# A transformer block, forward and backward: turning two chunks' attention outputs by DMA, two stores moved to ScalarE, and a new order

## The chip, the cores and the metric

The kernel runs on one core of a Trainium2 chip. The metric is the device time of one execution in microseconds. Three runs of the kernel before took 556.07, 557.82 and 574.06 us (median 557.82).

A core has five engines with a program each: TensorE (PE in the profile; its weight loads are PEld), VectorE (DVE), ScalarE (ACT), GpSimd (POOL) and SyncE (SP). They wait for each other by semaphores. A DMA is issued by SP, ScalarE or GpSimd and then carried out by 16 DMA engines.

## The reference

One pre-layernorm transformer block with 2048 positions of width 512, and the gradients of its input and six weights for a given output gradient. Attention has 32 heads of 16 and looks back at 8 positions, two apart. All tensors are bf16.

```python
def _A_ref(x, wqkv, wo):                       # S=2048, D=512, H=32, Dh=16, W=8, dil=2
    q, k, v = qkv of (x @ wqkv), by head
    idx = pos[:, None] - off[None, :]          # off = arange(8) * 2; masked where idx < 0
    logits = einsum("bhsd,bhswd->bhsw", q, k[idx]) * Dh ** -0.5
    attn = softmax(logits)
    o = einsum("bhsw,bhswd->bhsd", attn, v[idx])
    return o @ wo
def _B_ref(x, w1, b1, w2, b2):                 # F=1792
    return gelu(x @ w1 + b1) @ w2 + b2
def f(x, ...):
    h = x + _A_ref(layernorm(x), wqkv, wo)
    return h + _B_ref(layernorm(h), w1, b1, w2, b2)
outputs: f, and vjp(f)(grad_out): the gradients of x, wqkv, wo, w1, b1, w2, b2
```

(The first lines of `_A_ref` are shortened to words.)

## The kernel before, in words

**Tiling.** The 2048 positions are four chunks of 512 (chunk 0 to 3). A chunk's tile has 128 partitions and four blocks of 512. Three parts follow each other and overlap. Part 1 is the attention forward by chunk (`p1_ln`, `p1_qkv`, `p1_attn`, `p1_o`, `p1_h`). Part 2 is the feed-forward, forward and backward (`p2_h`, `p2_out`, `p2_dg`, `p2_bwd`). Part 3 is the attention backward (`p3_go`, `p3_dots`, `p3_bands`, `p3_gl1`) and the weight gradients (`wg_ffn`), whose long accumulations fill TensorE between the others.

**The attention output.** For each chunk `p1_o` gathers shifted rows of v by DMA and multiplies them on VectorE by the attention weights, in four bands (product `prbo`, L518). TensorE sums each band (`bsum`, L527), ScalarE evicts the sum into the tile `ost` (L532). `ost` has positions on the partitions; the projection by `wo` (in `p1_h`) needs it turned, as `oT`. A chunk number c in the tuple `FMO` decides how:

```python
            if m % 2 and c not in FMO:
                turn(ost, oT, m // 2, "o")
        if c in FMO:
            turned(ost, oT, "o")
```

`turn` makes eight 128x128 transposes on TensorE (L543), half a tile, and one copy of 1024 columns on ScalarE (L297). `turned` issues one DMA transpose of the whole tile on SP (L291, `xload`). `FMO` is empty, so all four chunks are turned by TensorE. Other tiles are turned by DMA already: `ln1T`, `ln2T`, `goT`, `ghT` and some `gqkvT`. After `wo`, TensorE's result is added to x on VectorE (`h`, L747), normalised (`ln2`, ScalarE L381) and turned into `ln2T`, which the first feed-forward matmuls of that chunk read.

**Wide and narrow matmuls.** Some matmuls write 32 partitions each and come in fours, one for each quarter of the array: the band sums (`S` as weights, L487 and L527) and the projection to q and k (L626). All other long ones write 128. `mmul` can split such a wide one (L270) into four narrow ones (L268). `emit` decides it from the order alone:

```python
                if o.cls == 4:          # a step of wide matmuls that may be split
                    run.append(i)
                else:
                    if prev == 1 and o.cls == 1:     # narrow before the run and behind it
                        quad.update(run)
                    run, prev = [], o.cls
```

A transposing step is neither class (0), so a run beside one stays wide.

**What sets the order.** The functions do not issue instructions; they record steps (`op`) with what they read and write. Two tables at the end of the file then fix everything: `ORDER` lists the steps in the order of issue, from which each engine takes its own, and `HOMES` gives each buffer's place in SBUF or PSUM. Each engine runs its steps strictly in that order. DMA issues count as steps of the issuing engine, so a DMA that waits for its source holds up the issues behind it on SP. Issues also wait until one of eight completion semaphores, shared by SP and ScalarE, is free again.

**The end.** `p3_gl1` ends the layernorm backward of a chunk: VectorE writes `gx` (L570), and four DMAs of 128 KB store it (L287, tag `gxst`), all on SP. The last weight gradients (`wgsq`, of wqkv) are evicted by ScalarE (L297) and stored by DMAs that ScalarE issues.

Of the kernel before, what the change touches and what calls it, by code (L numbers as in the profile page):

```python
# [13 lines left out]
ACT = mybir.ActivationFunctionType  # L14
# [145 lines left out]
def kernel(  # L160
# [798 lines left out]
    def p3_gl1(c):  # L959
# [20 lines left out]
        for j, ap in enumerate(perm_rows(gxf[c * CH:(c + 1) * CH, :])):  # L980
            store(None, lambda ap=ap: ap, gx, lambda j=j: gx()[32 * j:32 * j + 32], 128, tag="gxst")
# [201 lines left out]
FMO = ()  # L1183
# [115 lines left out]
)  # L1299


# [28 lines left out]
```

## Time and profile before

| | |
|---|---|
| Three runs | 556.07, 557.82, 574.06 us |
| The profiled execution | 557.15 us; its span, from the first to the last instruction, 555.4 us |
| TensorE | 539.7 us busy (97%), 5568 matmuls |
| VectorE | 494.2 us (89%) |
| ScalarE | 324.2 us (58%) |
| GpSimd | 32.4 us (6%) |
| Granted TensorE clock | 0.999 |
| DMA | 126.40 MB, 228 GB/s on average |
| HBM | 55.74 MB read, 35.21 MB written |

Busy time is a share of the span. The profile models the ends of matmuls, so that a busy TensorE need not be at its peak pace. The profile's views used below are: the page's busy shares; the windows (busy time of each engine in a stretch of the span); the groups of instructions by line (count, total, mean, and the idle time before them with what ended it); the waits (who waited for whom); the timeline; the DMA issues with the time from issue to landing; and the chain of work that ended last.

### The profile page before, as it was taken

What the parts mean: (1) busy time and instruction counts of PE and PEld (TensorE: products, weight loads), DVE (VectorE), ACT (ScalarE), POOL (GpSimd) and SP (SyncE); (2) the same over time, 40 slices, a digit from 0 to 9 for tenths busy, and PEclk for the clock granted to TensorE, in tenths of its full rate; (3) what the DMA queues carried; (4) which work ended last, traced back from release to release, by engine and by line L of the source; (5) the groups of instructions that cost most, each with busy time, mean ns of one, the idle gap of its engine ahead of it and who ended that gap; (6) DMA issues with size and microseconds to landing.
All of it is one profiled execution on the core that took longest, in us unless ns stands there. A gap on an engine that the chain in (4) does not pass through costs nothing. (4 is left out here: it accounts for less than half of the span.)

```text
span 555.4 us, 13067 instructions
## 1 busy us (share of the span) xinstructions
PE 539.7 (97%) x5568; PEld 268.9 (48%) x5568; DVE 494.2 (89%) x648; ACT 324.2 (58%) x503; POOL 32.4 (6%) x38
## 2 busy tenths in 40 slices
PE   7999999999999999999999999999999998999995
PEld 4655554444444444444444444455455554555442
DVE  7999999999999999889885877789879998999992
ACT  4998699887999794996131324042324556633531
POOL 1610100021001000000000000000010001000000
PEclk9999999999999999999999999999999999999999
DMA  8898998975499617298999989999999999778237
GB/s 265 218 289 251 395 368 236 199 228 185 97 268 281 179 34 167 77 152 221 199 210 184 194 183 187 295 212 271 240 357 374 305 335 372 318 272 162 52 72 199
DMA packets 195306, 126.40 MB, mean 228 GB/s; under 512 B 149744, under 2 KB 190896, under 8 KB 193200
## 3 DMA queue, kind: packets, MB, share of 16 engines
q1 hardware_dynamic: 189760, 82.06, 64.5%
q0 software_dynamic: 3312, 41.42, 19.2%
q10 hardware_dynamic: 2176, 2.10, 1.2%
q8 instruction: 43, 0.70, 0.5%
q14 instruction: 15, 0.12, 0.1%
HBM read 55.74 MB, written 35.21 MB: 164 GB/s over the span
## 5 line engine op out<-in xcount | busy, mean ns | idle before, releaser
L270 PE MATMUL ps<-goT,w2T 128*128 128x512 bf16 x224 | 53.6, 379 | 0.8 <-DVE h2s L828 0.5
L270 PE MATMUL ps<-w1T,xb 128*128 128x512 bf16 x224 | 52.9, 379 | 0.0
L270 PE MATMUL ps<-w,gl 128*128 128x512 bf16 x216 | 50.5, 379 | 0.0
L297 ACT CAST wgs<-ps 128x512 bf16<-128x512 f32 (+1 forms) x30 | 16.2, 558 | 57.4 <-PE ps L268 35.7
L270 PE MATMUL ps<-ln2T,w 128*128 128x512 bf16 x188 | 44.2, 379 | 0.7 <-DVE xb L856 0.3
L774 ACT ACTIVATE xb<-ps,b1c 128x512 bf16<-128x512 f32 x56 | 35.7, 692 | 12.8 <-PE ps L270 12.5
L856 DVE SCALAR_TENSOR_TENSOR xb<-xb,ps 128x512 bf16<-128x512 bf16 x56 | 36.6, 685 | 6.2 <-PE ps L270 5.6
L518 DVE TENSOR_TENSOR prbq<-Rq,cfq 128x4096 bf16<-128x4096 bf16 x16 | 36.0, 2288 | 5.0 <-PE ps L487 1.7
L479 DVE TENSOR_TENSOR prb<-got,vw 128x4096 bf16<-128x4096 bf16 x16 | 36.3, 2282 | 2.7 <-PE ps L487 1.4
L518 DVE TENSOR_TENSOR prbv<-Rv,cfv 128x4096 bf16<-128x4096 bf16 x16 | 36.1, 2283 | 2.7 <-PE ps L268 1.8
L518 DVE TENSOR_TENSOR prbk<-Rk,cfk 128x4096 bf16<-128x4096 bf16 x16 | 36.1, 2283 | 0.7 <-PE ps L527 0.7
L518 DVE TENSOR_TENSOR prbo<-Ro,cfo 128x4096 bf16<-128x4096 bf16 x16 | 35.9, 2288 | 0.4 <-DMA k_d<-tmk 0.2
L479 DVE TENSOR_TENSOR prf<-qt,kt 128x4096 bf16<-128x4096 bf16 x16 | 35.5, 2275 | 0.0
L270 PEld LDWEIGHTS <-w2T 128*128 128x128 bf16 x224 | 21.8, 98 | 27.4 <-issue 2.0
L270 PEld LDWEIGHTS <-xb 128*128 128x128 bf16 x224 | 21.9, 98 | 26.4
L270 PEld LDWEIGHTS <-gl 128*128 128x128 bf16 x216 | 20.8, 98 | 25.6 <-issue 1.6
L796 ACT ACTIVATE xb<-xb 128x2048 bf16<-128x2048 bf16 (+1 forms) x16 | 26.8, 1690 | 7.8 <-DVE xb L795 7.7
L626 PE MATMUL ps<-ln1T,wqk 128*32 128x512 bf16 x512 | 30.2, 383 | 0.0
L270 PEld LDWEIGHTS <-w 128*128 128x128 bf16 x188 | 18.1, 97 | 23.0 <-issue 2.5
L268 PE MATMUL ps<-wqkvT,gqkvT 128*32 128x512 bf16 x448 | 27.4, 379 | 1.7 <-ACT gqkvT L297 1.6
L777 ACT ACTIVATE gl<-xb 128x2048 bf16<-128x2048 bf16 (+1 forms) x16 | 26.8, 1697 | 0.0
L792 ACT ACTIVATE x<-xb 128x2048 bf16<-128x2048 bf16 (+1 forms) x16 | 26.6, 1690 | 0.0
(198 smaller groups left out, 1054.0 us busy)
## 6 DMA issues: line engine op xcount, KB each, us to landing
Ro<-v_d POOLq DMA_DIRECT2D x4, 2304.0 KB, 11.2
Rq<-k_d POOLq DMA_DIRECT2D x4, 2304.0 KB, 11.6
Rv<-go_d POOLq DMA_DIRECT2D x4, 2304.0 KB, 14.2
Rk<-q_d POOLq DMA_DIRECT2D x4, 2304.0 KB, 13.4
g_d<-gl SPq DMA_DIRECT2D x9, 512.0 KB, 3.5
gh_d<-xb SPq DMA_DIRECT2D x9, 512.0 KB, 3.4
w<-in_B_w_dram SPq DMA_DIRECT2D x2, 1792.0 KB, 15.0
out_dram<-wgs SPq DMA_DIRECT2D x13, 256.0 KB, 7.1
```

The source lines that it names most:

```text
L268: T.matmul(out[32 * a:32 * a + 32, :], lhsT=l[:, 32 * a:32 * a + 32], rhs=r, start=start, stop=stop, skip_group_check=True)
L270: T.matmul(out, lhsT=l, rhs=r, start=start, stop=stop, skip_group_check=True)
L297: fn = lambda: A.copy(out=ap(), in_=pap())
L479: op("DVE", tt_us(4096), lambda g=g, pr=pr: V.tensor_tensor(out=pr(), in0=ql()[:, g, :].unsqueeze(1).to_broadcast([P, W, 512]), in1=_sub(k ...
L518: V.tensor_tensor(out=pr().rearrange("p a j (d h) -> p a j d h", h=H), in0=_sub(R()[:, o0, 0:1], [[st, 2], [512, 4], [32, DH], [1, H]]), i ...
L626: T.matmul(ps()[32 * a:32 * a + 32, gg * 512:(gg + 1) * 512], lhsT=_sub(wq_()[:, dc, 0:1], [[DH, H]], sel * D + 4 * g + a), rhs=rhs, start ...
L774: op("ACT", act_us(512, 1), lambda f=f, ps=ps, xb=xb, f0=f0: A.activation(out=xb()[:, f - f0, :], in_=ps(), func=ACT.Identity, bias=b1c[:, ...
L777: op("ACT", act_us(N), lambda xb=xb, gl=gl: A.activation(out=fl(gl), in_=fl(xb), func=ACT.Gelu_apprx_tanh), r=[xb], w=[gl], tag="gelu", mo ...
L792: op("ACT", act_us(N), lambda xb=xb, x2=x2: A.activation(out=fl(x2), in_=fl(xb), func=ACT.Square), r=[xb], w=[x2], tag="x2")
L796: op("ACT", act_us(N), lambda xb=xb: A.activation(out=fl(xb), in_=fl(xb), func=ACT.Tanh, scale=GC), w=[xb], tag="tanh", mode=6)
L856: op("DVE", 0.61, lambda f=f, ps=ps, z=z, f0=f0: V.scalar_tensor_tensor(out=z()[:, f - f0, :], in0=z()[:, f - f0, :], scalar=1.0, in1=ps() ...
```

## The change

Three edits. `FMO` names chunks 1 and 3, so that their `ost` is turned by one DMA transpose each. Of chunk 3's four `gx` stores the second and the fourth are issued by ScalarE. `ORDER` and `HOMES` are new throughout (in each of the two chunks one DMA takes the place of two turns and two copies, so the program has six steps fewer and the numbers in the table mean other steps).

```diff
         for j, ap in enumerate(perm_rows(gxf[c * CH:(c + 1) * CH, :])):
-            store(None, lambda ap=ap: ap, gx, lambda j=j: gx()[32 * j:32 * j + 32], 128, tag="gxst")
+            store(None, lambda ap=ap: ap, gx, lambda j=j: gx()[32 * j:32 * j + 32], 128, q="ACT" if c == NC - 1 and j % 2 else "SP", tag="gxst")
...
-FMO = ()
+FMO = (1, 3)
...
 ORDER = (
-    8, 22, 0, 11, 12, 23, 1, 7, 10, 6, 9, 48, 364, 27, 13, 49, 50, 26, 51, 44, 61, 28, 2, 62, 40, 25, 3, 45, 29, 41, 24, 46, 52, 42, 43, 53, 363, 15,
+    8, 22, 23, 10, 0, 1, 9, 21, 12, 14, 15, 7, 18, 6, 48, 27, 26, 11, 49, 50, 28, 51, 61, 25, 2, 62, 29, 3, 19, 4, 24, 5, 467, 139, 52, 44, 53, 40,
...
 HOMES = (
-    1210, 96, 3159, 673, 2261, 2549, 1153, 1025, 2485, 2261, 2117, 336, 160, 3031, 2775, 224, 3031, 2967, 1665, 3095, 377, 1537, 2839, 160, 2912, 0,
+    1637, 449, 64, 673, 2261, 2549, 1153, 288, 2485, 2261, 2117, 272, 1989, 1985, 3031, 224, 3095, 1729, 3031, 416, 192, 128, 417, 2837, 737, 7, 673,
...
```

What this does to the engines is seen in their rows, here at three places. A row has the line, the instruction, what it writes and reads, and the size; the numbers in names tell buffers apart.

TensorE behind the last band sum of chunk 3's attention output (`prbo` and `S`), where the feed-forward stretch begins. Before, `w` is the first feed-forward weight, `w2T` the turned second one:

```order
L527 LDWEIGHTS S
L527 MATMUL ps<-prbo_41_2197,S 32x512
L270 LDWEIGHTS w_226_24_984
L270 MATMUL ps<-ln2T_533_38_2030,w_226_24_984 128x512
L270 LDWEIGHTS w_226_24_984
```

And now, at the same place:

```order
L527 LDWEIGHTS S
L527 MATMUL ps<-prbo_40_2261,S 32x512
L268 LDWEIGHTS w2T_29_1652
L268 MATMUL ps<-goT_25_1513,w2T_29_1652 32x512
L268 LDWEIGHTS w2T_29_1652
```

The matmuls behind the band sum were wide (L270) and are now narrow (L268). It stays so through the rest of the feed-forward part, up to the first narrow sums of part 3, since no transposing step stands between any more. Over the whole program the narrow matmuls go from 3728 to 6736, the wide ones from 1374 to 622, and the 128x128 ones from 400 to 368; PE's matmuls go from 5568 to 7792. The changes from wide to narrow or back, counted in the order, go from 46 to 32.

SP's queue about chunk 2's and chunk 1's `ln2T` (`w2T` are the turned weights, `goT` the turned output gradient, `k_d`, `q_d`, `g_d` stores to scratch). Before:

```order
L291 DMA_TRANSPOSE w2T_30_1496<-in_B_w_dram 128x4x448
L287 DMA k_d<-tmk_29_866 128x2x512
L287 DMA g_d_73<-gl_31_1721 128x2x512
L282 DMA xp_386_32_1568<-in_A_x_dram 32x4x512
L291 DMA_TRANSPOSE ln2T_478_34_1913<-ln_2_465_34_1879 128x16x128
L287 DMA k_d<-tmk_23_538 128x2x512
L1114 DMA r_d<-rtr 16x32
L291 DMA_TRANSPOSE ln2T_533_38_2030<-ln_1_520_37_2003 128x16x128
```

And now:

```order
L291 DMA_TRANSPOSE w2T_29_1652<-in_B_w_dram 128x4x448 x3
L1074 DMA k_d<-zrow 16x512
L287 DMA k_d<-tmk_28_1462 128x2x512
L291 DMA_TRANSPOSE oT_442_30_1903<-ost_35_1809 128x16x128
L291 DMA_TRANSPOSE ln2T_471_32_1975<-ln_2_457_30_1939 128x16x128
L287 DMA q_d<-tmq_30_1901 128x2x512
L287 DMA q_d<-tmq_32_1067 128x2x512
L287 DMA out_dram<-h2s_30_1937 128x1x512
L291 DMA_TRANSPOSE ln2T_522_37_2083<-ln_1_509_36_2056 128x16x128
```

Chunk 1's `oT` now comes from a DMA that stands right before chunk 2's `ln2T` and behind three of `w2T`'s four transposes.

ScalarE's last steps (`wgsq` is evicted and stored, `gx` is chunk 3's). Before:

```order
L287 DMA out_dram<-wgsq_36_6655 128x2x512
L297 CAST wgsq_14_7445<-ps 128x512
L287 DMA out_dram<-wgsq_14_7445 128x2x512
L297 CAST wgsq_6_7471<-ps 128x512
L287 DMA out_dram<-wgsq_34_7265 128x2x512
L297 CAST wgsq_6_7471<-ps 128x512
L287 DMA out_dram<-wgsq_6_7471 128x2x512
```

And now:

```order
L297 CAST wgsq_11_9673<-ps 128x512
L287 DMA out_dram<-gx_20_9623 128x1x512 x2
L297 CAST wgsq_7_9692<-ps 128x512
L297 CAST wgsq_11_9673<-ps 128x512
L287 DMA out_dram<-wgsq_11_9673 128x2x512
L297 CAST wgsq_7_9692<-ps 128x512
L287 DMA out_dram<-wgsq_7_9692 128x2x512
```

Two `gx` stores now stand on ScalarE before its last three evictions; SP's list of `gx` stores has 14 entries instead of 16.

200 rows, old and new, of tables (HOMES, ORDER) are left out of this document.

## The prediction

> **What bounds the kernel now.** I read the busy shares of the page first, then the stretches of the span, then who waits for whom.
>
> ```profile
> PE 539.7 (97%) x5568; PEld 268.9 (48%) x5568; DVE 494.2 (89%) x648; ACT 324.2 (58%) x503; POOL 32.4 (6%) x38
> PEclk9999999999999999999999999999999999999999
> 0.00:60.00 60.00, 57.17 (x724) 33.44 (x724) 55.03 (x78) 47.09 (x64) 15.40 (x15) 1.00 0.89 266
> 60.00:125.00 65.00, 61.34 (x649) 31.33 (x648) 62.68 (x74) 56.51 (x67) 5.04 (x5) 1.00 0.92 277
> 125.00:320.00 195.00, 193.82 (x1120) 87.75 (x1122) 174.24 (x328) 130.88 (x187) 3.92 (x3) 1.00 0.78 175
> 320.00:440.00 120.00, 119.61 (x1571) 62.06 (x1567) 101.06 (x68) 39.22 (x78) 4.31 (x8) 1.00 1.04 266
> 440.00:549.10 109.10, 107.40 (x1520) 54.31 (x1509) 101.16 (x104) 49.95 (x109) 3.70 (x7) 1.00 0.75 232
> ```
>
> TensorE is busy 97% of the span at the full granted clock. The stretches (columns: PE, PEld, DVE, ACT, POOL, clock, DMA share, GB/s) say where the rest is lost: 6.5 us of the first 125 (2.83 + 3.66), then 1.2 us in 195, 0.4 us in 120, 1.7 us in 109. After 125 us nothing but TensorE's own work sets the pace. Before it TensorE and VectorE are both nearly full, so a wait there can have either cause.
>
> A busy TensorE may still be slower than its pace, so I take the pace from the timeline of PE (start, length, and the count of matmuls merged into the row; successive starts give the pace).
>
> ```profile
> 49.29 2.81 PE L626 MATMUL ps<-ln1T,wqk 128*32 128x512 bf16 x48
> 52.04 0.62 PE L543 MATMUL ps<-ident,ost 128*128 128x128 bf16 x8
> 52.59 0.61 PE L487 MATMUL ps<-prf,S 128*32 128x512 bf16 x8
> ...
> 115.47 0.61 PE L543 MATMUL ps<-ident,ost 128*128 128x128 bf16 x8
> 115.92 1.46 PE L270 MATMUL ps<-w,gl 128*128 128x512 bf16 x6
> ...
> 147.58 0.61 PE L527 MATMUL ps<-prbo,S 128*32 128x512 bf16 x8
> 148.13 1.04 PE L270 MATMUL ps<-ln2T,w 128*128 128x512 bf16 x4
> 149.00 1.03 PE L270 MATMUL ps<-goT,w2T 128*128 128x512 bf16 x4
> ...
> 380.50 1.03 PE L270 MATMUL ps<-gw1in,ln 128*128 128x512 bf16 x4
> 381.46 0.62 PE L527 MATMUL ps<-prbq,S 128*32 128x512 bf16 x8
> ...
> 383.63 1.90 PE L268 MATMUL ps<-gw1in,ln 128*32 128x512 bf16 x32
> 385.36 0.60 PE L527 MATMUL ps<-prbq,S 128*32 128x512 bf16 x8
> ```
>
> Four wide matmuls (128 columns) take 0.87 us from 148.13 to 149.00, so 0.216 us each. Thirty-two narrow ones (32 columns) take 1.73 us from 383.63 to 385.36: 0.054 us each, and four of them 0.216, the same as the wide one they stand for. A turn, eight 128x128 transposes, takes 0.45 us (115.47 to 115.92). Where the width changes something more is lost: four wide ones take 0.96 us before narrow ones (380.50 to 381.46), 0.10 too many, and eight narrow ones 0.55 us before wide ones (147.58 to 148.13), 0.12 too many. I take 0.11 us per change of width. The program has 3728 narrow, 1374 wide, 64 half-length and 400 transposing matmuls; at these paces (0.11 for a half-length one) that is 201 + 297 + 7 + 22 = 527 us of the 548 between the first matmul (1.2) and the last. The other 21 us are 46 changes of width (5.1), the cold start, and waits.
>
> **The change part by part.**
>
> *Turns that leave TensorE.* Four turns go (two in chunk 1, two in chunk 3): 4 x 0.45 = **1.8 us** off a saturated engine. Their four copies on ScalarE go too:
>
> ```profile
> L297 ACT COPY oT<-ps 128x1024 bf16<-128x1024 bf16 x8 | 8.1, 1011 | 0.8 <-PE ps L543 0.7
> ```
>
> That is 4.0 us of ScalarE, which idles 42% of the span; I count nothing for it.
>
> *Fewer changes of width.* A turn is wide, and a run of wide matmuls is split into narrow ones only if nothing else stands between two narrow neighbours. Without the turns the new order has 32 changes instead of 46: 14 x 0.11 = **1.5 us**. The price is that 752 wide matmuls become 3008 narrow ones, nearly all of them in the feed-forward stretch (about 125 to 320 us). I count the conversion at zero, from the paces above. A row of the same stage and operands, split already, has no waiting in it either:
>
> ```profile
> L268 PE MATMUL ps<-ln2T,w 128*32 128x512 bf16 x144 | 8.6, 379 | 0.0
> L270 PEld LDWEIGHTS <-w2T 128*128 128x128 bf16 x224 | 21.8, 98 | 27.4 <-issue 2.0
> L268 PEld LDWEIGHTS <-gqkvT 128*32 128x32 bf16 x448 | 12.2, 97 | 14.1 <-ACT gqkvT L297 2.1 <-DMA gqkvT<-gks 0.6
> ```
>
> Loading 32 columns takes 97 ns, as long as loading 128 (98 ns). If the four loads of a split matmul ran one after another, they would take 4 x 97 = 388 ns, more than its 216; but 448 of them together occupy 12.2 us, 27 ns each, since they overlap. The cost lies between 0 (the streamed columns are the same, which excludes a gain) and 172 ns a piece; I take 0, because the measured rows are split ones. The Trainium skill states a rule against this change, in "TensorEngine Tiling (Array Packing)", Restrictions and Gotchas: column tiling excludes the fast weight load. The equal 97 and 98 ns agree with it. By that rule alone, with loads in series, the sum would become 683 us; by the trace's pace it is unchanged.
>
> *Two DMA transposes that come in.* Chunk 1's and chunk 3's tile is now turned on SP's queue, and the `wo` matmuls wait for the landing. The changed order puts 30 wide equivalents (6.5 us) between chunk 1's last band sum and `wo`, and 36 (7.8 us) for chunk 3. ScalarE's eviction of that sum comes first:
>
> ```profile
> L532 ACT ACTIVATE ost<-ps 128x512 bf16<-128x512 f32 x16 | 9.3, 599 | 1.4 <-PE ps L527 1.4
> ln2T<-ln SPq DMA_TRANSPOSE x3, 4.3
> ghT<-ghr SPq DMA_TRANSPOSE x4, 9.0
> gqkvT<-gqs SPq DMA_TRANSPOSE x1, 11.9
> 352.97 13.57 DMA ghT<-ghr
> ```
>
> The same shape lands 4.3 us after issue for ln2T, which is turned in this very stretch, and 13.57 us after it in the worst case of the trace (the chain, at 353 us, with the DMA engines full). With 0.6 for the eviction, 4.9 us fits under 6.5 and 7.8: no wait. With 13.57 the waits are 7.7 and 6.4 us. I take zero, since ln2T is nearest in place; both ends are kept. A gain below zero is excluded, as these matmuls stood behind the turns before. Behind the new issue on SP stands chunk 2's ln2T, whose source, the normalised rows, comes later on ScalarE than the turned tile's last eviction; so the queue does not hold it up; behind chunk 3's stand w1T's, first needed well after that `wo`. The two transposes move 1 MB more, at a DMA share of 0.78 to 0.92 there.
>
> *The last stores.*
>
> ```profile
> 545.86 5.67 SPq L287 DMA_DIRECT2D out_dram<-gx  x6
> ...
> 549.50 0.58 ACT L297 CAST wgsq<-ps 128x512 bf16<-128x512 f32 x1 [1.14 <-PE ps L270]
> 550.12 0.38 ACTq L287 DMA_DIRECT2D out_dram<-wgsq  x1
> DMA to landing us min/median/max: 2.4/2.5/3.7
> ```
>
> SP issues its last gx store by 551.53, ScalarE its last wgsq store at 550.12, and stores land 2.4 to 3.7 us after issue. So both end between 552.5 and 554. Taking two of 16 issues from SP frees some 1.2 us there (0.6 each), but the wgsq store, which follows the last matmul, ends as late: I count 0, between -0.5 and +1. On ScalarE the two issues (0.38 each) stand before three evictions; the last one had waited 1.14 us for TensorE and so covers 0.76, if gx is ready. The Trainium skill's "DMA: Bandwidth & Descriptors", Issuing engines are not separate DMA queues, says a second issuing engine saves only the issuing time; with these rows that saving is hidden too, so rule and rows both give 0.
>
> *The new order elsewhere.* Its gain or loss is what becomes of TensorE's waits. Those that the view of waits lists on PE add up to about 8 us: these are the largest but for the start.
>
> ```profile
> PE ps L268 <- ACT gqkvT L297: 1.6, 1, 1.6
> PE ps L416 <- DVE ln L385: 1.5, 1, 1.5
> PE ps L270 <- DVE h2s L828: 1.4, 2, 0.9
> PE ps L416 <- ACT kt L297: 1.0, 1, 1.0
> ```
>
> They can go (-8) or double (+8). I take 0.
>
> **Sum.** The profiled execution took 557.15 us, 1.75 beyond its span of 555.4 and 0.7 below the median shown (557.82). 557.15 - 1.8 - 1.5 = **553.9 us**.
>
> **The rivals.**
>
> *VectorE paces the first stage (555.8).* Up to 145 us it lacks little:
>
> ```profile
> DVE st L360 <- DMA xt<-in_A_x_dram: 1.7, 1, 1.7
> DVE nm L376 <- POOL rstd L373: 1.6, 3, 0.9
> ```
>
> If TensorE's savings there only make it wait for VectorE's products, 9 of the 14 changes of width (1.0 us) and chunk 1's turns (0.9) are given back: 553.9 + 1.9. For it: VectorE's work is the same as before. Against it: the loss of 6.5 us there has other causes as well.
>
> *The turned tiles land late, and the kernel is slower (558.8 to 568).* It decides from a landing of 5.9 us for chunk 1 and 7.2 for chunk 3; from 8.2 us for both the two waits eat the gain of 3.3. With ghT's median of 9.0 they are 3.1 and 1.8: 553.9 + 4.9 = 558.8; with 13.57 they are 14.1: 568. For it: the DMA share of 0.92, and w2T's transposes queued just ahead on SP. Against it: ln2T's 4.3.
>
> *The split matmuls do not keep pace (683).* 752 x 0.172 = 129 us more. Only the single load time speaks for it.
>
> *The early waits shrink as well.* Half of the 8 us gone gives 549.9, all of it 545.9.
>
> **How the numbers follow.** Forecast 0.60 (own range 551.5 to 556), VectorE 0.15, late tiles 0.12, shrinking waits 0.10, split matmuls 0.03. Two per cent, about what a measurement of this kernel can tell from no change, is 546.0 and 568.3 around 557.15. Below lies only the far end of the shrinking waits, with 0.05 for what the new order may do unseen; above lie the split matmuls and the worst landings, 0.05. The range from 548 to 562 leaves out the tails of both, under 2 in 10.
>
> **What would show it.** Right: PE's transposing rows of ost fall from 64 to 32; the narrow pace in 125 to 320 us stays at 0.054 us with no idle time; PE's `wo` rows wait for no oT transpose; the last matmul starts some 3 us earlier; what follows it stays near 6 us. Wrong: a PE wait on oT of over 2 us, a pace of 0.058 or more in the feed-forward stretch (0.004 x 4 x 900 matmuls is 14 us, the 2% alone), or waits in the first 145 us that differ by more than 3 us from 6.5. What I cannot read from the profile is how a wholly new order meets the DMA queue early on: that would make the prediction wrong first.

## The result, and the profile after

The changed kernel took 562.42 us (median of 20 runs, 558.06 to 569.32), the kernel before 556.91 in the same comparison (20 runs, 553.87 to 574.06): a ratio of **1.0059**, 95% interval 1.0035 to 1.0084. A second comparison gave 565.71 against 556.00, 1.0118 (1.0064 to 1.0172). So the change costs 0.6 to 1.2%, where 0.6% less was forecast. The changed kernel's own times stand in two groups, 558 to 564 and 566 to 569 us, and the profile below is of an execution of 567.36 us. The ratios and intervals, here and below, leave out runs more than 1.5% above the fastest of their kernel (of the changed kernel the whole upper group); the medians count all.

The page of the changed kernel (busy shares, granted clock, instruction queue), then its stretches in the columns of before (length, PE, PEld, DVE, ACT, POOL, clock, DMA share, GB/s):

```profile
PE 541.3 (96%) x7792; PEld 286.5 (51%) x7792; DVE 496.4 (88%) x648; ACT 321.8 (57%) x499; POOL 25.2 (4%) x38
PEclk9999999999999999999999999999899999999999
q8 instruction: 61, 1.00, 0.8%
```

```profile
0.00:60.00 60.00, 55.88 (x709) 35.45 (x710) 55.57 (x76) 45.77 (x63) 8.54 (x15) 1.00 0.88 267
60.00:125.00 65.00, 63.14 (x736) 32.66 (x734) 62.46 (x74) 55.52 (x66) 4.67 (x5) 1.00 0.98 268
125.00:320.00 195.00, 188.45 (x3247) 98.98 (x3249) 171.28 (x329) 131.17 (x190) 3.94 (x3) 0.99 0.84 177
320.00:440.00 120.00, 113.35 (x1437) 58.54 (x1433) 91.00 (x61) 31.43 (x58) 3.78 (x7) 0.99 1.04 252
```

The first 125 us lost 6.5 us of TensorE before and lose 5.98 now. The loss is new, and later: 6.55 us in 125 to 320 us (1.2 before) and 6.65 in 320 to 440 (0.4 before). A shorter execution (561.01 us, gx_all_SP below) still loses 6.97 and 4.02 there. The view of waits on PE names what ended them (total, times, longest), and the timeline shows the two longest (idle time before a row, and its releaser, in brackets):

```profile
PE ps L487 <- ACT wgs L297: 4.2, 1, 4.2
PE ps L268 <- DVE xb L856: 3.7, 2, 3.3
PE ps L487 <- DVE prb L479: 1.8, 2, 1.0
```

```profile
266.13 1.90 PE L268 MATMUL ps<-w1T,xb 128*32 128x512 bf16 x16 [3.33 <-DVE xb L856]
...
386.30 0.54 POOL L471 DMA_DIRECT2D Rv<-go_d  x1 [38.66 <-ACT got L297]
386.44 1.60 SPq L287 DMA_DIRECT2D out_dram<-wgs  x3
...
398.54 0.58 ACT L297 CAST wgs<-ps 128x512 bf16<-128x512 f32 x1 [8.79 <-DMA out_dram<-wgs]
399.17 0.62 PE L487 MATMUL ps<-prb,S 128*32 128x512 bf16 x4 [4.16 <-ACT wgs L297]
```

Each of the two costs more than its length. Right behind it the granted clock is about half (third column from the right), though the page's row of tenths hardly shows it:

```profile
266.20:269.60 3.40, 3.40 (x36) 1.43 (x39) 3.30 (x6) 3.13 (x3) 0.00 (x0) 0.53 0.76 259
399.20:402.60 3.40, 3.40 (x36) 1.46 (x39) 2.29 (x1) 0.62 (x2) 0.00 (x0) 0.51 0.77 205
```

TensorE is busy for all of the 3.40 us, and by the clock 1.6 us of them are lost each time, on top of waits of 3.33 and 4.16. The Trainium skill's "TensorE: Matmul & The Clock Gate", Part 1: The HAM clock gate, says that the array falls to half its clock after an idle window of about 3.4 us and gets it back after as long a busy one. The 3.4 us agree; but the window need not be idle here, as the last section shows from all profiles.

### The profile page after: what moved, and what is told of

It is laid out like the page before. It is cut to its first block, busy times and chain, and to the rows that moved or that the text cites. A ratio compares the mean times of both kernels' runs of the same rounds, so it can differ in the third digit from the quotient of the medians.

```text
span 565.6 us, 17518 instructions
## 1 busy us (share of the span) xinstructions
PE 541.3 (96%) x7792; PEld 286.5 (51%) x7792; DVE 496.4 (88%) x648; ACT 321.8 (57%) x499; POOL 25.2 (4%) x38
## 4 chain that ended last, share of the span: by engine, by line
PE 41%; DMA 5%; DVE 4%; SPq 2%; ACT 1%; issue 0%; DVEq 0%; ACTq 0%
PE ps L268 22%; PE ps L270 14%; PE ps L527 3%; DMA out_dram<-wgs 2%; DMA ln1b<-ln_d 2%; DVE prbv L518 2%; SPq L291 1%; DVE prb L479 1%; PE ps L543 1%; DMA tmgod<-got 1%; DVE prbk L518 1%; PE ps L487 1%; ACT got L297 0%; PE ps L919 0%; DVE h L755 0%
## 5 line engine op out<-in xcount | busy, mean ns | idle before, releaser
L268 PE MATMUL ps<-w1T,xb 128*32 128x512 bf16 x896 | 53.0, 383 | 3.5 <-DVE xb L856 3.3
L268 PE MATMUL ps<-goT,w2T 128*32 128x512 bf16 x832 | 52.0, 379 | 1.1 <-DVE xb L856 0.4
L268 PE MATMUL ps<-w,gl 128*32 128x512 bf16 x776 | 46.2, 384 | 0.0
L268 PEld LDWEIGHTS <-xb 128*32 128x32 bf16 x896 | 26.2, 98 | 26.5 <-issue 4.6
L268 PEld LDWEIGHTS <-w2T 128*32 128x32 bf16 x832 | 24.4, 97 | 22.6 <-issue 2.2
L561 ACT ACTIVATE gyr<-ps,rstd 128x512 bf16<-128x512 f32 x16 | 10.9, 680 | 39.4 <-PE ps L268 39.4
L268 PEld LDWEIGHTS <-gl 128*32 128x32 bf16 x776 | 23.0, 98 | 20.2 <-issue 1.4
L268 PE MATMUL ps<-ln2T,w 128*32 128x512 bf16 x512 | 31.1, 379 | 0.6 <-DMA w<-in_B_w_dram 0.3
L268 PE MATMUL ps<-gor,gw2in 128*32 128x512 bf16 x416 | 24.8, 379 | 0.7 <-DMA gw2in<-g_d 0.7
```

The source lines that it names most:

```text
L268: T.matmul(out[32 * a:32 * a + 32, :], lhsT=l[:, 32 * a:32 * a + 32], rhs=r, start=start, stop=stop, skip_group_check=True)
```

## The experiments

All were timed beside the kernel before; medians in us, and the ratio to before with its 95% interval:

| kernel | median | before | ratio |
|---|---|---|---|
| again (the changed kernel) | 565.71 | 556.00 | 1.0118 (1.0064–1.0172) |
| gx_all_SP | 566.36 | 556.00 | 1.0147 (1.0104–1.0190) |
| woT_copy_later | 569.30 | 556.00 | 1.0229 (1.0179–1.0279) |
| wgs_home | 571.80 | 556.00 | 1.0274 (1.0241–1.0306) |
| store_before_gather | 563.48 | 555.72 | 1.0115 (1.0088–1.0142) |
| store_and_woT | 564.95 | 555.72 | 1.0150 (1.0093–1.0208) |
| change_in_old_order | 573.53 | 555.72 | 1.0270 (1.0211–1.0329) |
| long_run_wide | 556.95 | 555.72 | 1.0009 (0.9981–1.0038) |
| split_in_old_kernel | 558.62 | 556.00 | 1.0043 (1.0023–1.0062) |
| split_first_part | 557.23 | 556.00 | 1.0034 (1.0010–1.0059) |
| split_last_part | 560.41 | 556.00 | 1.0093 (1.0062–1.0124) |
| cut_by_columns | 562.39 | 556.68 | 1.0102 (1.0066–1.0138) |
| wide_store_copy | 556.47 | 556.00 | 1.0007 (0.9979–1.0034) |
| wide_store_copy_junk | 554.87 | 556.68 | 0.9985 (0.9953–1.0017) |
| old_order_wide | 568.69 | 556.68 | 1.0199 (1.0167–1.0230) |
| four_waits_wide | 554.31 | 555.87 | 0.9970 (0.9954–0.9986) |
| four_waits_split | 563.71 | 555.87 | 1.0102 (1.0065–1.0140) |

**First theory: the waits of the new order.** Nothing edited, and the stores on ScalarE undone:

> The changed kernel once more, nothing altered; its times so far lie between 558 and 569 us, and the profile that we have is of an execution of 567.4. Theory A (waits of the new order): TensorE waits 3.66 us at 262 us for VectorE's xb products and 4.48 us at 395 us behind an eviction that waits for a weight gradient store, and runs at half rate for about 2.5 us after each; an execution of about 559 us should show the same two waits, and be shorter because one or both stay below the length from which the half rate follows, or because the clock granted elsewhere is higher. Theory B (the parts of the change themselves): a shorter execution shows neither wait, and is still 2 us or more above the kernel before; then the loss is spread over the narrow matmuls or the tail.

```diff
-... q="ACT" if c == NC - 1 and j % 2 else "SP", tag="gxst")
+... tag="gxst")
```

> The changed kernel with all four of the last chunk's input gradient stores issued by SyncE again; order and homes as in the changed kernel. Theory A: the stores on ScalarE are worth nothing, so the time stays within 1 us of the changed kernel. Theory B: the two stores on ScalarE cost (or gain) 2 us or more, and the time moves by that.

The second profile of the changed kernel (568.94 us) has the waits at 262 and 395 us again, 3.3 and 5.1 us. With all stores on SyncE the profiled execution took 561.01 us; it has the first wait, but not the second. There the store was issued ahead of the gather:

```profile
384.06 1.64 SPq L287 DMA_DIRECT2D out_dram<-wgs  x3
384.64 0.54 POOL L471 DMA_DIRECT2D Rv<-go_d  x1 [38.66 <-ACT got L297]
392.32 0.58 ACT L297 CAST wgs<-ps 128x512 bf16<-128x512 f32 x1 [4.24 <-PE ps L268]
```

It landed at 388.63, 4.6 us after issue; in the changed kernel it was issued 0.14 us behind the gather and landed with it, 12.0 us later (398.46 and 398.11). The time of the kernel can't be told from the changed one's (566.36 and 565.71 in one comparison).

**Two of the waits taken apart.** ScalarE's copy moved back, and another place for one staging buffer:

```diff
 ScalarE: sums of goT, tanh, tanh
-COPY woT<-woR          (ahead of them)
+COPY woT<-woR          (behind the last tanh)
 SyncE:   ... gh_d<-xb, gh_d<-xb
+DMA_TRANSPOSE xw2in<-gl (was ahead of these two)
```

> The changed kernel with ScalarE's 4.04 us copy of woT, which starts at 257.06 us between the small steps that VectorE waits for, moved behind the third tanh step that follows it, into ScalarE's idle stretch of 7.69 us (269.3 to 277.0); one transposing load of gl that takes over its source's place moves with it. Theory A: VectorE no longer sits 2.73 us at 263.3 behind ScalarE, TensorE's wait of 3.66 us at 262 us shrinks below 1 us and the half rate after it goes, so the kernel gains 3 to 6 us on the changed one (553 to 556 us). Rival: VectorE was late by its own load, the wait stays at 2.5 us or more, and the time stays within 1.5 us of the changed kernel.

```diff
 HOMES, entry of one wgs buffer
-2085
+0
```

> The changed kernel with one staging buffer of the weight gradients (the one that ScalarE fills at 398.5 us) in another place of SBUF, so that it no longer waits for the store of the buffer that lay there (issued at 386.4, landed at 398.5 us). Theory A: ScalarE's 8.8 us wait and TensorE's 4.48 us behind it go, with the half rate after it: a gain of 4 to 7 us (552 to 555 us). Rival: the gather issued at 386.3 us, which lands at 398.1, is what really holds that stretch: TensorE then waits for VectorE's products or ScalarE's taps at the same place, and less than 1.5 us is gained.

Both kernels became slower, as neither theory had it. The waits aimed at went, and what stood behind them was worse. In the first, VectorE now waited for the transfer that had moved along, whose source its next junk output overwrites; in the second it waited for the same late store, whose place it now shared (views of waits on VectorE, one row of each kernel):

```profile
DVE jk L564 <- DMA xw2in<-gl: 6.4, 1, 6.4
```

```profile
DVE cfv L497 <- DMA out_dram<-wgs: 12.8, 1, 12.8
```

TensorE waited 6.4 us at 269 us and 8.2 us at 418 us instead. In both it was then VectorE that waited for a transfer. So the store was moved on its queue:

```diff
 SyncE
+out_dram<-wgs
 DMA_TRANSPOSE gw1in<-gh_d   (2.41 us)
-out_dram<-wgs
```

> The changed kernel with one weight gradient store (the 256 KB one that lands last at 398.5 us in the profile after) moved one place ahead on SyncE's queue, before the transposing load that holds that queue for 2.41 us, so that it is always issued ahead of the 2304 KB gather that GpSimd issues at 386.3 us. Theory A: whether this store is issued just before or just after the gather makes the two groups of the changed kernel's times: 384.06 before 384.64, landed after 4.6 us, in an execution of 561.0 (the kernel with all stores on SyncE); 386.44 after 386.30, landed after 12.0 us, in one of 567.4. Then all times here lie at 558 to 561 us and TensorE waits less than 1 us at 394 to 400 us. Rival: the two groups come from the clock; then times of 565 and more stay as frequent as they are in the changed kernel (about half).

> The kernel with the store ahead of the gather, and ScalarE's 4.04 us copy of woT in its idle stretch as in woT_copy_later, but with the transposing load that takes its source's place put behind the small loads of r_d on SyncE's queue, so that nothing which VectorE needs stands behind it (there VectorE sat 6.4 us for them). Theory A: TensorE's wait of 3.65 us at 262 us goes together with the half rate after it (1.5 to 2.6 us): 552 to 556 us, 3 to 6 below store_before_gather. Rival: VectorE is late by its own work there and at least 2 us of the wait stay: within 2 us of store_before_gather.

In store_before_gather TensorE no longer waits at 394 us, but the times still reach from 558 to 575 us: the rival's side, as far as the times go. Its profile (563.68 us) has a wait of 3.3 us at 418 us, for the next pair of that kind: a store of go_d, issued 0.39 us ahead of the next gather, landed 11.8 us later. (The row there names a store of wgs; in wide_store_copy_junk, where the same eviction waits, it names that of go_d.) store_and_woT missed likewise: VectorE waited 7.5 us for xw2in<-gl once more. Over all profiles the first pair is consistent: in each of the nine in which the store of wgs was issued first, TensorE did not wait for that eviction; in each of the five in which the gather was (the changed kernel twice, and later woT_copy_later, long_run_wide and split_first_part), it waited 3.5 to 5.1 us. In long_run_wide the way is longer: behind the gather the issue of a transposing load took 8.80 us, and the store stood behind it on SyncE's queue. (wgs_home, where that eviction no longer waits for the store, is left out.)

**The change without its order, and without its split.**

```diff
-FMO = ()
+FMO = (1, 3)
+... q="ACT" if c == NC - 1 and j % 2 else "SP", tag="gxst")   (order of before, 20 steps of chunk 1 moved back)
```

> The kernel before with the change's two named parts alone: the attention outputs of chunks 1 and 3 turned by a DMA transpose in place of TensorE, two of the last four input gradient stores issued by ScalarE. Order and places are those of before, but for 20 steps of chunk 1 that follow its turned tile (its DMA, the four output projections, the additions and layer norm behind them), which stand some 20 to 40 places later, so that the 4 to 7 us of the DMA have cover. Theory A: the parts are worth what the prediction said, the order is what lost it: 551.5 to 554.5 us where before has 556. Rival: the parts themselves cost: 556 us or more.

```diff
-                    if prev == 1 and o.cls == 1:
+                    if prev == 1 and o.cls == 1 and len(run) < 100:
```

> The changed kernel, in which the one long run of 188 matmul steps (125 to 320 us) that was split into narrow matmuls is left wide: 752 matmuls of 128 columns in place of 3008 of 32. Theory A: the split costs nothing, and the time stays within 1.5 us of the changed kernel (two more changes of width, 0.2 us). Rival: 3008 small matmuls hold TensorE up (their instructions, their weight loads): the time falls by 3 us or more.

In both the rival held. The parts, in the old order and with the 20 steps moved, cost 2.7%. And leaving one run wide, which I had counted at nothing twice, brought the changed kernel back to the kernel before: 1.0009. The split became the main suspect, and came next: in the kernel before, in each part of the run, and cut in another direction.

```diff
 split_in_old_kernel (in before)
-                    if prev == 1 and o.cls == 1:
+                    if (prev == 1 or at[i] == 1190) and o.cls == 1:
 split_first_part, split_last_part (in after)
-                        quad.update(run)
+                        quad.update(x for x in run if len(run) < 100 or at[x] < 1030)     (last: >= 1030)
```

> The kernel before, order and places untouched; only its long run of 163 wide matmul steps (652 matmuls, behind the last turn of chunk 3's outputs up to the first part 3 sums, some 165 to 330 us) is split into 2608 narrow ones, as the changed kernel's long run is. Theory C (the split costs, not by TensorE's own pace but by DMA: in the changed kernel the transposing loads at 264 to 336 us land after a median of 5.6 to 6.0 us, in the same kernel with the run left wide after 4.7 to 4.9, and the queue that brings instructions moves 61 packets in place of 42): 2 to 5 us slower than before, with later transposing loads in that stretch. Rival, my prediction's step: the pace of four narrow matmuls is that of one wide, so within 1 us of before.

> The changed kernel in which the long run of 188 steps is narrow in its first 120 steps (125 to about 260 us) and wide in the last 68. Theory C: SyncE's queue is not the limit there (its transfers have gaps), so the time is that of the kernel with the run left wide, 556 to 558 us. Rival D: every narrow matmul costs the same somewhere on TensorE or its weight loads, so 120 of 188 steps cost 64% of what the split costs (2.4 of 558.8 against 556.9 in the shorter runs, 5 to 6 by the medians): 558 to 561 us.

> The same the other way round: the first 120 steps wide, the last 68 (about 260 to 320 us, where SyncE issues transposing loads one behind the other) narrow. Theory C: nearly the whole cost of the split, 559 to 563 us. Rival D: 36% of it, 557.5 to 559 us.

The split costs 0.43% in the kernel before, whose order and places are untouched. In the changed kernel its first 120 steps cost nothing that can be told (557.23 against 556.95 with the run wide; 1.0034 and 1.0009) and its last 68 cost 3.5 us (560.41). A price per matmul would have put 64% on the first part, so that rival is out; the cost sits where SyncE issues transposing loads back to back. There the loads land later (issues of 264 to 336 us in the wide kernel, the changed kernel, and split_last_part; count, median us to landing; ahead of them the queues' packets, MB, and share of 16 engines):

```profile
q1 hardware_dynamic: 52051, 14.41, 102.5%
q8 instruction: 3, 0.05, 0.3%
xw1in<-xb SPq DMA_TRANSPOSE x4, 4.8
ghT<-ghr SPq DMA_TRANSPOSE x3, 4.7
vw<-v_d SPq DMA_TRANSPOSE x2, 4.7
```

```profile
q1 hardware_dynamic: 48353, 13.47, 113.2%
q8 instruction: 10, 0.16, 1.0%
xw1in<-xb SPq DMA_TRANSPOSE x4, 5.3
ghT<-ghr SPq DMA_TRANSPOSE x3, 5.6
vw<-v_d SPq DMA_TRANSPOSE x2, 5.6
```

```profile
q8 instruction: 9, 0.15, 0.9%
xw1in<-xb SPq DMA_TRANSPOSE x4, 6.3
ghT<-ghr SPq DMA_TRANSPOSE x3, 6.4
vw<-v_d SPq DMA_TRANSPOSE x2, 5.0
```

The split kernels move less in more time, and their instruction queue brings 9 or 10 packets there in place of 3. Groups of three or four scatter (the kernel before has 5.4 for its xw1in), but the mean of all transposing loads issued in this stretch, 16 to 18 in each kernel, sorts all nineteen profiles: 4.6 to 4.9 us in the seven in which the stretch is wide, 5.0 to 5.7 in the twelve in which it is split.

Who pays for it can be read too (waits on VectorE, the changed kernel, then the wide one, whose list has no `tmgod`):

```profile
DVE prb L479 <- DMA xw1in<-xb: 3.0, 1, 3.0
DVE u L566 <- DMA tmgod<-got: 2.4, 1, 2.4
```

```profile
DVE prb L479 <- DMA xw1in<-xb: 0.3, 1, 0.3
```

SyncE issues the first of these `tmgod` at 329.73 us in place of 325.01. In the nine profiles of the new order with the last part narrow, VectorE waits 2.1 to 3.4 us for `tmgod`, and TensorE 0.7 to 2.8 for VectorE's `prb` in the same stretch; of the five with it wide four have at most 0.5 and none, one (four_waits_wide, below) 1.8 and 1.1. split_in_old_kernel has later loads (5.05 us in the mean, before 4.80) but no such wait: where its 2.4 us go is not shown, and its profile is of a run of 556.58 us, below its median.

Is it the number of instructions, or the narrow tile?

```diff
 cut_by_columns: the last 68 steps, four matmuls each
-T.matmul(out[32 * a:32 * a + 32, :], lhsT=l[:, 32 * a:32 * a + 32], rhs=r, ...)
+T.matmul(out[:, 128 * a:128 * a + 128], lhsT=l, rhs=r[:, 128 * a:128 * a + 128], ...)
```

> The kernel split_last_part with another cut: the last 68 steps of the long run (260 to 320 us) are again four matmuls each in place of one, but cut along the 512 moving columns (four times 128 x 128 weights on 128 columns), so that the array stays full width; the first 120 steps are wide. As many more instructions as in split_last_part. Theory C1 (the number of instructions that TensorE must be brought delays the transposing loads): the loads land after 5 to 6.4 us as there, and the time is 559 to 563 us, of which 1.6 us are the slower pace itself (4 x 0.0555 us against 0.2158, 272 times). Theory C2 (narrow tiles themselves): loads at 4.4 to 5.0 us as in the kernel left wide, 557 to 559 us.

In this kernel some partial sums of those steps are not kept; number and size of the instructions are as described. Its time, 562.39 us less 1.6 for the pace (an estimate, from 0.0555 us a piece against a quarter of 0.2158), is near that of split_last_part (560.41), and its loads land as late (means 5.2 and 5.2 us):

```profile
q8 instruction: 9, 0.15, 0.9%
xw1in<-xb SPq DMA_TRANSPOSE x4, 5.3
ghT<-ghr SPq DMA_TRANSPOSE x3, 6.1
vw<-v_d SPq DMA_TRANSPOSE x2, 5.4
```

So the number of instructions delays the loads, not the narrow tile (C1). That it costs the whole time is likely from the times but not shown by this trace: its profile, of 560.09 us, has no wait of VectorE for `tmgod` and 1.4 us for xw1in. By which path the instructions delay the loads is not shown either: that their packets stand in the loads' way on the DMA engines fits the rows, but was not tried by itself. The Trainium skill's "DMA: Bandwidth & Descriptors", Queues, rings and completion order, says that an engine takes turns between queues a whole packet at a time; a packet of instructions here holds 16 KB (1.00 MB in 61). No run here isolates that.

**The old order again, with the run wide.** The edit is that of long_run_wide in change_in_old_order.

> The kernel change_in_old_order (the change's two parts in the order of before, 573.5 us) with its long run left wide. The split was worth 2.4 us in the kernel before. Theory: 569 to 572 us, and the waits for the turned tiles (5.0 and 4.6 us and the half rate after them) remain, so it is they, not the split, that make that kernel slow. Rival: the split is the main cost there too: 560 us or less.

568.69 us, as expected: the split is the smaller part there. TensorE waits for the turned tile of chunk 3 and for chunk 1's layer norm, which my edit had delayed along with its turned tile:

```profile
PE ps L270 <- DMA ln2T<-ln: 6.1, 2, 5.9
PE ps L270 <- DMA oT<-ost: 5.7, 2, 4.2
```

So the new order does buy something: cover for chunk 3's turn at least; the wait for the layer norm comes at least in part from my own edit.

**The waits taken away together.** With the run wide:

```diff
 ScalarE
-COPY woT<-woR
 c x4, sums of goT x2, tanh
+COPY woT<-woR
```

> The changed kernel with three edits: the long run left wide; the weight gradient store ahead of the transposing load on SyncE's queue (as in store_before_gather); and ScalarE's 4.04 us copy of woT put between two small groups of its steps so that VectorE's next inputs (five 0.2 us steps, two sums, one 1.9 us tanh) come ahead of it, with no transfer moved past another that VectorE needs. If the three waits named so far are what the change lost: the wait of 3.4 us at 261 us shrinks below 1.5 us and the one at 390 us goes, 551 to 555 us, below both kernels. Rival: what is next late (VectorE's own load of 88%) takes the place of the wait, 556 to 558 us.

```diff
 HOMES, two jk buffers
-1409, 1825
+1841, 416
```

> The kernel wide_store_copy (556.5 us), in which VectorE sat 2.2 us at 267 us until a transposing load had read a tile whose place its next junk output takes; the two junk outputs there have another place now. If that wait was the last of that stretch, TensorE's wait of 2.4 us at 267 us and its half rate after it (1.8 us) go: 552 to 554 us, below both kernels. Rival: another wait of VectorE takes its place, 555.5 to 557 us.

```diff
 SyncE
+go_d<-tmgod
 DMA_TRANSPOSE gw1in<-gh_d
-go_d<-tmgod
```

> The kernel wide_store_copy_junk (554.9 us), in whose profile one wait of more than 2 us is left behind the start: 2.9 us at 413 us, for an eviction that waits for a store of go_d issued at 401.95 us, 0.33 us after a gather of 2304 KB, and landed with it at 413.7. Here that store goes ahead of one transposing load on SyncE's queue, some 3 us earlier. If the rule of the other store holds (ahead of the gather it lands in 4 to 5 us, behind it in 12): no wait of TensorE above 1 us at 405 to 420 us in the profile, times of 552 to 554 us, below both kernels. Rival: the load that now comes later is waited for, or another transfer takes the place: 554.5 to 556.5 us.

> The same kernel with the long run split as in the changed kernel: the changed kernel with the four waits taken out and nothing else. The split was worth 2.4 us in the kernel before and 3.5 to 5.5 in the changed one. Theory: it costs 2 to 4 us against four_waits_wide, 554.5 to 557.5 us, so that the waits and the split add up to what the change lost. Rival: without the waits, the late loads have cover and the split costs nothing: within 1 us of four_waits_wide.

wide_store_copy missed its 551 to 555 us: TensorE's wait at 262 us shrank to 0.5 us, and one of 2.2 us came at 267, VectorE waiting 2.2 us for xw2in<-gl. Without that the median fell to 554.87 (1.8 us below before, not yet told from no change), and with the last edit to 554.31: **0.9970 (0.9954 to 0.9986), the one version faster than both kernels**. The last edit itself gained nothing that can be told, 554.87 to 554.31. Its profile, of an execution of 560.98 us (ten of its other twelve runs took less than 555.4), has the rival's wait: 3.8 us for the load that was moved back.

```profile
PE ps L268 <- DMA gw1in<-gh_d: 3.8, 1, 3.8
PE ps L270 <- DMA oT<-ost: 1.7, 1, 1.7
```

With the split put back the same kernel takes 563.71 us, 1.0102. That is more than the 2 to 4 us expected, and the rival (cover without the waits) is out. In its profile late loads are now what TensorE waits for longest. But that execution took 558.38 us, less than the one profiled of four_waits_wide, so these rows do not account for the 9 us between the medians:

```profile
PE ps L268 <- DMA ghT<-ghr: 2.3, 1, 2.3
PE ps L487 <- DVE prb L479: 1.9, 2, 1.2
```

## Why the prediction was wrong

**The step that failed first is "I count the conversion at zero, from the paces above".** The pace was right: in the changed kernel 112 narrow matmuls of the run that was split take 6.04 us from start to start, 0.054 each.

```profile
185.79 6.23 PE L268 MATMUL ps<-w1T,xb 128*32 128x512 bf16 x112
191.83 1.05 PE L268 MATMUL ps<-goT,w2T 128*32 128x512 bf16 x16
```

But both bounds, 0 and 172 ns a piece, were prices on TensorE, and what the runs show is a price beside it: 3008 matmuls in place of 752 have to be brought, the transposing loads beside them land 0.25 to 0.9 us later in the mean, and in the new order VectorE, and behind it TensorE, waits for them. It measured 0.4% of the kernel before (2.4 us), 0.5 to 1.1% between the changed kernel and long_run_wide, and 1.3% between the two kernels of four waits (1.0102 against 0.9970). I had quoted the wide and narrow rows of PE and PEld, and none of the DMA queues in that stretch. The split is a result of the change itself: the turn of chunk 3 stood between two narrow neighbours and kept that run wide.

**The second is "The new order elsewhere ... I take 0".** With the run wide, the four edits to the waits brought 1.0009 to 0.9970, 2.2 us. My sentence that "after 125 us nothing but TensorE's own work sets the pace" was read from the old order and carried over to one in which VectorE, ScalarE and two pairs of transfers stand closer: 13.2 of 315 us are lost there now in the long execution and 11.0 in the shorter one, 1.6 before; part of this is the split's. The half clock behind long waits was in no term at all.

Point by point for the rest:

- *Turns, 1.8 us.* Right in its count: PE's transposing rows of ost are 32, before 64.

```profile
L543 PE MATMUL ps<-ident,ost 128*128 128x128 bf16 x32 | 2.3, 220 | 0.0
```

- *The turned tiles.* Wait near zero, as forecast, but not for the reason given: both landed after 6.7 us, longer than the 4.3 that I took, and TensorE's weight loads waited 0.5 us; in four_waits_wide it was 1.7 (view of the tile oT: durations of the issues, then the landings). The rival's point (5.9 us for chunk 1) was passed by 0.8. In the old order the same turns cost 4.2 us in one wait: the rival was real, and the new order is what kept it small.

```profile
L291 SPq DMA_TRANSPOSE oT<-ost x2: 1942/2794/3646, 110.4 to 148.1; - x2
...
DMA to landing us min/median/max: 6.7/6.7/6.7
```

- *The last stores.* From the last issue of wgsq to the end of the span the changed kernel takes 4.3 us (561.27 to 565.6), with all stores on SyncE 5.7 (553.53 to 559.2), before 5.3. About 1 us is gained in the tail, a little beyond my range; in the times it can't be told. My rows had allowed it: with landings of 2.4 to 3.7 us SP's last store could come in as late as 554.6, ScalarE's by 553.8, so the two did not end together at 554.

```profile
561.27 0.39 ACTq L287 DMA_DIRECT2D out_dram<-wgsq  x1
```

- *The sum.* With the run wide and four waits edited, the kernel gains 1.6 us (554.31 against 555.87; 0.14 to 0.46% by the interval), where turns and changes of width were counted at 3.3 us, 0.6%. So half of the count is seen, and some of that can be the edits' own; what each of the two terms is worth was not measured. That 554.31 lies beside the forecast 553.9 is luck, since that was counted from 557.15.
- *The rivals.* "VectorE paces the first stage" was not it: the loss of the first 125 us hardly changed (6.5 to 5.98), which is also all that the early waits shrank. "The split matmuls do not keep pace" named the right part with the wrong place, and so a price of 129 us in place of 2 to 7. The closing sentence, that I could not read how a new order meets the DMA queue, looked early in the span; it was late.
- *The signs.* None of the three signs of being wrong came: the wait on oT was 0.5 us, the pace 0.054, and the first 145 us lost 7.3 us where before lost 6.7. No sign stood on the loads of the feed-forward stretch, or on waits behind 145 us.
- *Still open:* by which path more instructions delay the loads; where the split's cost goes in the old order; and why single executions differ by some us in the order in which a store and a gather are issued.

## What to carry to other kernels

Price an edit that multiplies instructions on the queues that bring data as well as on the engine that runs them: read the landing times of the loads beside it, and ask who waits for them. When an order is replaced, list the pairs of transfers that stand within a microsecond of each other on different queues, and each small step that queues behind a long one; a margin that was safe in the old order says nothing of the new one. And a wait of TensorE can cost another 1.7 us of half clock behind it: count how much of each 3.41 us it leaves busy, not only how long it is.

## What the hardware showed that I had not expected

- A store of 256 KB issued 0.58 us ahead of a gather of 2304 KB landed after 4.6 us; issued 0.14 us behind it, after 12.0 us. Being ahead is not always enough: the store of go_d went 0.39 us ahead of its gather and landed after 11.8 us.
- 1632 more instructions for TensorE in 60 us (816 matmuls and their weight loads) went with a median landing of xw1in's and ghT's transposing loads of 6.3 and 6.4 us in place of 4.8 and 4.7 (vw's 5.0 and 4.7; the mean of all sixteen 5.2 and 4.8), with TensorE's own pace unchanged.
- The granted clock follows the busy time of fixed stretches, not the length of a wait. In all nineteen profiles it changes only in steps of 3.41 us, counted from its first rise. Cut along that grid (up to 545 us), each of the 28 stretches at full clock in which TensorE was busy for at most 1.35 us was followed by half the clock, and none in which it was busy for 1.36 or more; full clock came back behind a stretch with 2.74 us busy or more, not behind one with 2.55 or less. (Ends of matmuls are modelled, so the borders are estimates.) So wide_store_copy's wait of 2.2 us was followed by half clock, as its windows show, while wgs_home's of 3.3 us at 268 us, which left 1.36 us busy, and one of 3.55 us in store_and_woT, spread over two stretches, were not.

```profile
266.67:270.08 3.41, 1.18 (x6) 0.48 (x5) 2.50 (x7) 1.26 (x5) 0.00 (x0) 1.00 1.03 321
270.08:273.49 3.41, 3.41 (x10) 1.22 (x8) 3.38 (x8) 0.00 (x0) 0.00 (x0) 0.50 1.00 212
```
